# A fused attention and gated-MLP block on one core: first loads in another order, six split projections, and a new instruction order

## The chip, the cores and the metric

The kernel runs on one NeuronCore of a Trainium2 chip. The metric is device time in microseconds for one launch. Names of engines: PE is the matrix engine (PEld its weight loads), DVE the vector engine, ACT the scalar engine, POOL GpSimd, SP the engine that issues most transfers. ACT can issue transfers too.

## The reference

Sequence 2048, width 512, all in bf16. `layernorm` has no scale or shift.

```python
q, k, v = split(layernorm(x) @ wqkv)            # 32 heads of 16
# each position looks at 8 keys: itself and 2, 4, ..., 14 positions back
logits = einsum("bhsd,bhswd->bhsw", q, k_gathered) * 16 ** -0.5
attn = softmax(where(idx >= 0, logits, -1e9))
h = x + einsum("bhsw,bhswd->bhsd", attn, v_gathered) @ wo
g = layernorm(h) @ W_gate                        # 512 -> 1376
return h + (relu(g) * (layernorm(h) @ W_up)) @ W_down
```

## The kernel before, in words

The sequence is cut into four chunks (tk = 0 to 3) of 512 rows, each of four blocks of 128 rows. All weights and x stay in on-chip memory once loaded (`x_sm`, `wqk_sb`, `wv_sb`, `wo_sb`, `wgu_sb`, `wd_sb`). A chunk passes these steps; the letters are the keys of the steps in the code, with a chunk's number behind a dot in the text.

- Layer norm of x: `xst` and `xag` (statistics and aggregate on DVE, L454 and L457), `xrl` and `xre` (two small steps on ACT, L467 and L471), `xn` (normalised rows, DVE, L489), `xtp` (four 128-column transposes per block on PE, L518), `xte` or `xtv` (copy out of the accumulator bank, on ACT L534 or DVE L532). In chunk 0 each block goes through this by itself; blocks 0 and 2 are copied by ACT, 1 and 3 by DVE.
- Projections: twelve outputs of 128 x 512 (four each of q, k, v), each of four matmuls over the depth of 512 (`dt` = 0 to 3, L559), and a copy by ACT (`qe`, L567).
- Scores: DVE multiplies q with shifted k (`pr`, L608, in halves in chunk 0, L623), PE sums within heads (`sc`, L614), ACT takes the exponential, PE sums the denominators (`den`). The weights are spread over the head's rows by transfers on SP (`bd`, L732; on PE, `bc`, L743, in chunk 0).
- Values: DVE multiplies with shifted v (`mu`, L764, L779), an accumulating transfer issued by POOL adds the upper to the lower half (`ta`, L807; in chunk 3 DVE does this), DVE adds the rest (`tree`, L767, L801; `om`, L771, in chunk 0). The result is OT; PE multiplies with wo (`wo`, L833), the sum with x goes back into `x_sm` (`rs`).
- Second layer norm (`hnm`, `hsq`, `hrl`, `hre`, `hxn`) with transposes on PE (`htp`) or by transfers on SP (`htd`, L507).
- MLP: up and gate matmuls (`mm`, L906), copies on ACT (`ue` L910, `ge` L913), a product on DVE (`gu`, L934), the down projection (`dn`, L952), a last sum with x (`o`, L963) and the store (`os`).

All these steps are recorded first (`plan.add`) with their engine, what they depend on and the buffers that they take. `Plan.order` then lists them engine by engine: `RANK` gives each of the 737 steps its place, and a planner, with a duration for each step and a landing time for each load (`xload`, `wload`), decides what is written next; two pairs in `GUIDE` add dependences between first-chunk statistics. The engines run their lists in order, and every wait is by semaphore. The planner's numbers decide only the order.

The first loads are issued by hand in `setup`. x of chunk 0 goes in four pieces of 128 KB, the q, k weights in four pieces of 256 KB (one for each `dt`), half of each on SP and half on ACT. POOL holds back a later load by writing one element into its destination, in an instruction that reads an earlier load: `wv_sb` waits in that way for the first x (L326), chunk 2 for chunk 1 (L328).

Before the first transposes PE runs `NWARM` matmuls on a zero tile (L408), and after those of blocks of the first half `NFILL` more (L416). The first four projections of chunk 0 are cut in three pieces each: columns 0 to 255 over the first half of the depth (`qka`), columns 256 to 511 over the first half (`qkc`), all columns over the second half (`qkd`).

```python
f_mm(lo, hi, 0, 2)      # qka and qkc: two matmuls of 256 columns
f_mm(0, CS, 2, NT)      # qkd: two matmuls of 512 columns
```

Of the kernel before, what the change touches and what calls it, by code (L numbers as in the profile page):

```python
# [16 lines left out]

RANK = [
    0, 1, 2, 3, 4, 5, 6, 7, 8, 9, 10, 11, 12, 13, 14, 15, 16, 17, 19, 20,
    25, 27, 32, 39, 18, 21, 23, 24, 26, 30, 40, 42, 29, 34, 36, 37, 41, 43, 46, 22,  # L20
    28, 31, 33, 35, 38, 44, 49, 53, 56, 66, 47, 60, 71, 85, 48, 54, 58, 62, 45, 50,
    51, 55, 77, 82, 72, 78, 81, 101, 68, 89, 100, 110, 61, 69, 96, 102, 94, 114, 107, 70,
    116, 111, 126, 135, 145, 99, 74, 95, 105, 112, 117, 120, 169, 183, 196, 149, 164, 156, 153, 159,
    123, 133, 138, 130, 128, 207, 199, 213, 234, 237, 241, 185, 162, 191, 223, 233, 240, 189, 194, 200,
    230, 235, 238, 170, 147, 176, 203, 211, 220, 250, 258, 256, 261, 246, 252, 243, 248, 266, 276, 264,
    273, 267, 271, 263, 269, 279, 282, 286, 290, 289, 292, 296, 293, 297, 291, 294, 300, 330, 335, 319,
    321, 308, 312, 316, 323, 338, 353, 357, 340, 355, 334, 342, 343, 360, 364, 304, 309, 325, 328, 314,
    333, 310, 336, 348, 356, 365, 337, 347, 349, 362, 327, 345, 367, 346, 384, 359, 371, 368, 377, 363,
    369, 388, 376, 382, 392, 373, 386, 390, 402, 381, 431, 450, 465, 415, 445, 475, 489, 403, 429, 459,
    466, 411, 424, 448, 485, 67, 73, 59, 65, 52, 64, 57, 63, 75, 76, 83, 88, 79, 86, 93,  # L30
    80, 91, 84, 90, 97, 174, 198, 157, 168, 142, 195, 172, 206, 151, 179, 106, 109, 115, 122, 132,
    221, 136, 143, 108, 118, 103, 113, 119, 125, 215, 225, 232, 254, 242, 249, 260, 265, 274, 278, 281,
    284, 295, 288, 302, 322, 332, 358, 370, 331, 339, 372, 383, 341, 350, 380, 385, 317, 324, 361, 378,
    397, 406, 393, 396, 395, 400, 389, 394, 408, 410, 399, 405, 404, 407, 398, 401, 412, 413, 418, 421,
    414, 417, 419, 423, 416, 422, 425, 436, 439, 438, 444, 457, 481, 447, 472, 488, 451, 462, 432, 442,
    443, 460, 453, 458, 464, 461, 469, 476, 487, 474, 478, 468, 483, 490, 486, 493, 482, 491, 463, 495,
    514, 519, 523, 522, 527, 524, 535, 508, 533, 504, 536, 539, 513, 532, 544, 517, 530, 547, 549, 541,
    582, 647, 681, 543, 607, 616, 678, 531, 614, 624, 649, 537, 634, 638, 724, 87, 104, 124, 144, 129,
    139, 131, 137, 152, 163, 177, 182, 175, 180, 186, 181, 187, 178, 188, 192, 201, 210, 227, 229, 253,
    259, 226, 247, 222, 231, 208, 245, 239, 244, 205, 214, 228, 251, 277, 311, 270, 374, 285, 344, 298,  # L40
    275, 315, 318, 268, 257, 280, 326, 352, 354, 366, 375, 387, 379, 391, 440, 449, 480, 484, 427, 434,
    456, 479, 420, 428, 454, 467, 433, 441, 471, 477, 499, 507, 492, 496, 497, 502, 494, 498, 510, 512,
    500, 503, 505, 509, 501, 506, 515, 516, 525, 538, 528, 534, 518, 521, 520, 526, 566, 570, 557, 571,
    569, 581, 604, 608, 613, 563, 567, 575, 580, 561, 564, 573, 583, 585, 546, 551, 556, 558, 550, 555,
    553, 560, 565, 628, 630, 601, 611, 621, 626, 618, 622, 633, 625, 639, 597, 632, 578, 588, 610, 637,
    644, 631, 635, 643, 629, 640, 641, 645, 667, 670, 673, 676, 658, 688, 716, 721, 636, 669, 671, 674,
    684, 685, 694, 723, 134, 140, 121, 127, 92, 98, 141, 146, 148, 150, 160, 166, 155, 165, 173, 154,
    161, 158, 167, 171, 262, 283, 184, 209, 236, 303, 190, 204, 272, 287, 217, 219, 218, 255, 197, 202,
    212, 224, 301, 305, 299, 307, 193, 216, 313, 306, 320, 329, 409, 351, 426, 430, 435, 437, 446, 452,
    470, 455, 473, 529, 540, 545, 552, 554, 568, 572, 579, 511, 562, 574, 577, 542, 548, 559, 576, 584,  # L50
    587, 586, 591, 589, 595, 593, 599, 590, 592, 594, 596, 598, 600, 602, 603, 605, 606, 620, 623, 609,
    612, 615, 617, 619, 627, 642, 656, 680, 683, 675, 691, 648, 661, 692, 682, 700, 687, 689, 696, 702,
    690, 697, 706, 654, 679, 664, 666, 665, 668, 672, 677, 686, 652, 660, 657, 659, 646, 650, 653, 655,
    662, 699, 710, 707, 709, 704, 713, 693, 711, 714, 651, 698, 701, 663, 695, 703, 705, 715, 717, 719,
    720, 708, 722, 726, 730, 718, 725, 728, 732, 729, 733, 735, 736, 712, 727, 731, 734,
]


# [33 lines left out]
class Plan:  # L92
# [18 lines left out]
        return op  # L111


    GUIDE = (("xag0", 0, "xst1", 0), ("xxn1", 0, "xst2", 0))

    def order(self):
        for kx, cx, ky, cy in self.GUIDE:
            xs = [o for o in self.ops if o.key and o.key[0].startswith(kx) and o.key[1] == cx]
            for o in self.ops:
                if o.key and o.key[0].startswith(ky) and o.key[1] == cy:  # L120
                    o.deps = o.deps + xs
        waiting = list(self.ops)
        free = {}
        queues = None
# [84 lines left out]
def kernel(  # L209
# [11 lines left out]
    nc = tc.nc  # L221
# [83 lines left out]
    def setup():  # L305

        w3_r = A_wqkv.rearrange("(dt p) f -> p dt f", p=P)
        for j in range(BPC):
            (nc.scalar if j % 2 else nc.sync).dma_start(x_sm[:, j:j + 1, :], x_rows[:, j:j + 1, :])
        for dt in range(NT):  # L310
            (nc.scalar if dt % 2 else nc.sync).dma_start(wqk_sb[:, dt:dt + 1, :], w3_r[:, dt:dt + 1, 0:2 * D])
        nc.sync.dma_start(x_sm[:, BPC:2 * BPC, :], x_rows[:, BPC:2 * BPC, :])
        nc.scalar.preload_act_table_set("natural_log_exp_and_others")
        V.memset(warm[:], 0.0)
        make_identity(nc, identity[:])
# [7 lines left out]
        nc.gpsimd.memset(vT[:, :, 0:PADL], 0.0)  # L323


        nc.gpsimd.tensor_copy(out=wv_sb[0:1, 0, 0:1], in_=x_sm[0:1, 0, 0:1])  # L326
        nc.sync.dma_start(wv_sb[:], w3_r[:, :, 2 * D:3 * D])
        nc.gpsimd.tensor_copy(out=x_sm[0:1, 2 * BPC, 0:1], in_=x_sm[0:1, BPC, 0:1])  # L328
        for tk in range(2, NCK):
# [33 lines left out]
    DAC2 = ()  # L363
    PRS, MUH = (0,), (0,)
    TDD, TDL = 1.25, 1.5
    NWARM, NFILL = 44, 8
    DMAT = (('h',2,0),('h',2,2),('h',3,0),('h',3,2),('h',1,0))

    EARLY = (1, 2, 3)
# [27 lines left out]
    def load(t):  # L397
        return add(None, "LD", 0.0, None, lat=t)

    xload = [[load(t) for t in (3.5, 3.7, 4.1, 4.35)]] + [[load(t)] * BPC for t in (10.8, 14.4, 17.8)]  # L400
    wload = {n: load(t) for n, t in
             (("q", 9.55), ("k", 9.55), ("ab", 8.1), ("v", 12.1), ("o", 19.2), ("u", 22.6), ("g", 26.1), ("d", 30.1))}

    wb = Buf(bank_s)

# [1 line left out]
        for _ in range(NWARM):  # L407
            nc.tensor.matmul(wb.t[:, 0:P], lhsT=warm[:], rhs=warm[:], start=True, stop=True)  # L408

    fills = [add(("warm", 0), "PE", 5.7, f_warm, [], -500, take=[wb])]  # L410

    def fill(d):

# [128 lines left out]
    for tk in range(NCK):  # L542
# [10 lines left out]
        for n, (c, t) in enumerate(seq):  # L553
            mm = Buf(mm_s)
            pr = base + 10 + 0.1 * n

            def f_mm(lo=0, hi=CS, d0=0, d1=NT, c=c, t=t, mm=mm, xnT=xnT):
                for dt in range(d0, d1):
                    nc.tensor.matmul(mm.t[:, lo:hi], lhsT=wv_sb[:, dt, t:D:NT] if c == 2 else wqk_sb[:, dt, c * D + t:(c + 1) * D:NT],  # L559
                                     rhs=xnT.t[:, dt, lo:hi], start=(dt == 0 and lo == 0), stop=(dt == NT - 1))  # L560

            def f_ev(c=c, t=t, mm=mm, qT=qT, s0=s0):
                if c == 0:
                    o = qT.t[:, t, :]
                else:
                    o = (kT if c == 1 else vT)[:, t, PADL + s0: PADL + s0 + CS]
                nc.scalar.copy(out=o, in_=mm.t[:])  # L567

            wl = wload["qkv"[c]]
            if tk == 0 and n < 4:  # L570

                ab, done = [wload["ab"]], []
                for i, (lo, hi, evs) in enumerate(((0, 2 * P, xev[0:2]), (2 * P, CS, xev[2:]))):
                    done.append(add(("qk%s%d" % ("ac"[i], n), tk), "PE", 2 * MM * (hi - lo) / CS + 0.005,
                                    lambda f=f_mm, lo=lo, hi=hi: f(lo, hi, 0, 2), evs + ab + done + [fills[-1]], pr - 5,
                                    take=[mm], use=[xnT]))
                a = add(("qkd%d" % n, tk), "PE", 2 * MM, lambda f=f_mm: f(0, CS, 2, NT), done + [wl], pr - 4.9, take=[mm],
                        use=[xnT], lat=PEL)
            else:
                a = add(("qkv%d" % n, tk), "PE", 4 * MM, f_mm, xev + [wl], pr, take=[mm], use=[xnT], lat=PEL)  # L580
            b = add(("qe%d" % n, tk), "ACT", A5, f_ev, [a], pr, take=[qT] if c == 0 else [], use=[mm], lat=AL)
            if c == 0:
                qd[t] = b
            elif c == 1:
                kdone[tk, t] = b
            else:
                vd[t] = b
# [434 lines left out]
```

## Time and profile before

| what | value |
|---|---|
| timed runs, median of 3 (lowest to highest) | 198.19 us (198.18 to 198.19) |
| span of the profiled execution, first to last instruction | 196.6 us |
| busy time of PE in the span | 190.5 us, 97% |
| busy time of DVE | 154.0 us, 78% |
| busy time of ACT | 111.7 us, 57% |
| granted clock of PE, mean | 1.000 |
| moved by transfers | 21.99 MB, mean 112 GB/s |
| start of the first projection matmul | 8.76 us |

The profile is of one execution; the timed runs are others of the same program, so the two are compared by differences. A busy PE counts matmuls that overlap, with modelled ends, so the pace of matmuls is taken from many of a kind in a row. In lines of the timeline the first two numbers are start and length in us, "x8" counts instructions, and the bracket tells how long the engine was idle ahead and what ended that.

### The profile page before, as it was taken

To read this page: it belongs to the slowest core of one execution; us is meant where nothing else is said; L and a number is where in the kernel's file an instruction comes from. 1 tells how busy PE (TensorE), PEld (TensorE's weight loads), DVE (VectorE), ACT (ScalarE), POOL (GpSimd) and SP (SyncE) were. 2 spreads that over 40 slices of the span, in tenths; PEclk is the share of its full clock that TensorE was granted. 3 is DMA by queue.
4 is the path that set the end of the run, shared out by engine and by line. 5 is a ranking of instruction groups with operands and counts; after the bars stand their busy time and mean duration, and the time that the engine had idled before them with its cause. 6 is when DMAs were issued, how large, how long until landed. Compare 5 with 4: busy or idle time off the path is not lost.

```text
span 196.6 us, 3034 instructions
## 1 busy us (share of the span) xinstructions
PE 190.5 (97%) x1111; PEld 97.1 (49%) x1131; DVE 154.0 (78%) x251; ACT 111.7 (57%) x234; POOL 12.7 (6%) x28
## 2 busy tenths in 40 slices
PE   7899999999999999999999999999999999999994
PEld 7756445654445434464444435444444655444542
DVE  6779999999999999999999779999686331223233
ACT  3548699984598947694334658505674615235400
POOL 4000000330000013100033000000000000000000
PEclk9999999999999999999999999999999999999999
DMA  6969980695000809947369971411002220030114
GB/s 154 310 202 389 405 262 2 122 198 108 3 0 6 196 15 173 188 89 169 81 130 198 181 204 64 82 29 24 3 0 53 53 57 0 0 107 0 27 57 133
DMA packets 21134, 21.99 MB, mean 112 GB/s; under 512 B 8736, under 2 KB 17920, under 8 KB 21120
## 3 DMA queue, kind: packets, MB, share of 16 engines
q1 hardware_dynamic: 18672, 14.65, 25.9%
q0 software_dynamic: 1728, 6.29, 17.2%
q10 hardware_dynamic: 720, 0.85, 1.4%
q8 instruction: 9, 0.15, 0.3%
q14 instruction: 5, 0.04, 0.1%
HBM read 8.42 MB, written 2.10 MB: 53 GB/s over the span
## 4 chain that ended last, share of the span: by engine, by line
PE 66%; DMA 14%; issue 13%; DVE 4%; POOL 1%; SPq 1%; POOLq 0%; DVEq 0%
PE bank L906 20%; PE bank L559 19%; PE bank L952 14%; DMA big<-big 7%; PE bank L833 5%; DMA wv_sb<-in_A_wqkv_dram 4%; PE bank L614 2%; DVE big L764 2%; PE bank L873 2%; PE bank L518 2%; DMA x_sm<-in_A_x_dram 1%; POOL big L807 1%; DMA big<-ex 1%; DVE big L608 1%; PE bank L836 1%
## 5 line engine op out<-in xcount | busy, mean ns | idle before, releaser
L906 PE MATMUL bank<-quad,wgu_sb 128*128 128x512 bf16 x313 | 72.0, 379 | 0.4
L906 PEld LDWEIGHTS <-wgu_sb 128*128 128x128 bf16 x320 | 31.0, 98 | 37.3 <-issue 0.8
L952 PE MATMUL bank<-wd_sb,gT 128*128 128x512 bf16 (+2 forms) x182 | 40.1, 366 | 0.3
L913 ACT ACTIVATE gr<-bank 128x512 bf16<-128x512 f32 x40 | 23.2, 603 | 26.0 <-PE bank L906 24.5
L910 ACT CAST up_sb<-bank 128x512 bf16<-128x512 f32 x40 | 23.2, 594 | 16.5 <-PE bank L906 14.0
L934 DVE TENSOR_TENSOR gT<-gr,up_sb 128x1024 bf16<-128x1024 bf16 x20 | 13.7, 689 | 22.7 <-ACT up_sb L910 16.8
L559 PE MATMUL bank<-quad,wqk_sb 128*128 128x512 bf16 (+1 forms) x132 | 30.2, 367 | 0.2
L952 PEld LDWEIGHTS <-gT 128*128 128x128 bf16 (+1 forms) x187 | 18.1, 98 | 19.5 <-issue 0.4
L764 DVE TENSOR_TENSOR big<-big,vT 128x4096 bf16<-128x4096 bf16 x12 | 27.0, 2283 | 0.1
L608 DVE TENSOR_TENSOR big<-quad,kT 128x4096 bf16<-128x4096 bf16 x12 | 27.0, 2284 | 0.0
L559 PEld LDWEIGHTS <-wqk_sb 128*128 128x128 bf16 x136 | 14.7, 114 | 13.0 <-issue 2.1
L963 DVE TENSOR_TENSOR row<-x_sm,bank 128x512 bf16<-128x512 bf16 (+1 forms) x17 | 10.8, 651 | 9.2 <-PE bank L952 9.2
L767 DVE TENSOR_TENSOR big<-big 128x1024 bf16<-128x1024 bf16 (+2 forms) x24 | 16.8, 729 | 1.2 <-DMA big<-big 1.2
L559 PE MATMUL bank<-quad,wv_sb 128*128 128x512 bf16 x62 | 15.7, 380 | 0.4 <-DMA wv_sb<-in_A_wqkv_dram 0.3
L807 POOL DMA_DIRECT2D big<-big x12 | 10.5, 874 | 85.0 <-DVE big L764 55.0
L833 PE MATMUL bank<-wo_sb,quad 128*128 128x512 bf16 x62 | 14.7, 379 | 0.4 <-DVE quad L801 0.3
L489 DVE TENSOR_SCALAR row<-x_sm,mv,rs 128x512 bf16<-128x512 bf16 x32 | 11.4, 407 | 1.8 <-ACT rs L471 1.8
L534 ACT COPY quad<-bank 128x1024 bf16<-128x1024 bf16 (+1 forms) x11 | 10.0, 944 | 4.5 <-PE bank L518 4.4
L567 ACT CAST kT<-bank 128x512 bf16<-128x512 f32 x16 | 8.9, 598 | 5.7 <-PE bank L559 5.5
L454 DVE BATCH_NORM_STATS2 st<-x_sm 128x6 f32<-128x512 bf16 x16 | 10.3, 675 | 2.1 <-DMA x_sm<-in_A_x_dram 2.1
L567 ACT CAST quad<-bank 128x512 bf16<-128x512 f32 x16 | 9.5, 607 | 3.6 <-PE bank L559 3.6
L443 ACT ACTIVATE row<-x_sm,mv 128x512 bf16<-128x512 bf16 x12 | 8.6, 714 | 4.2 <-DVE mv L435 4.0
(72 smaller groups left out, 157.5 us busy)
## 6 DMA issues: line engine op xcount, KB each, us to landing
big<-big POOLq DMA_DIRECT2D x12, 512.0 KB, 5.4
big<-ex SPq DMA_DIRECT2D x24, 128.0 KB, 2.7
out_dram<-row SPq DMA_DIRECT2D x15, 128.0 KB, 1.8
x_sm<-in_A_x_dram SPq DMA_DIRECT2D x3, 512.0 KB, 4.9
wgu_sb<-in_B_W_up_dram SPq DMA_DIRECT2D x1, 1376.0 KB, 8.8
wgu_sb<-in_B_W_gate_dram SPq DMA_DIRECT2D x1, 1376.0 KB, 11.8
wd_sb<-in_B_W_down_dram SPq DMA_DIRECT2D x1, 1280.0 KB, 15.2
wqk_sb<-in_A_wqkv_dram SPq DMA_DIRECT2D x2, 256.0 KB, 6.9
```

What stands on the lines that cost most here:

```text
L559: nc.tensor.matmul(mm.t[:, lo:hi], lhsT=wv_sb[:, dt, t:D:NT] if c == 2 else wqk_sb[:, dt, c * D + t:(c + 1) * D:NT], rhs=xnT.t[:, dt, lo:h ...
L567: nc.scalar.copy(out=o, in_=mm.t[:])
L608: V.tensor_tensor(out=pb.t[:].rearrange("p (t w) s -> p t w s", t=2), in0=q4, in1=k4, op=ALU.mult)
L764: V.tensor_tensor(out=mt.t[:], in0=ab.t[:], in1=v8, op=ALU.mult)
L767: V.tensor_tensor(out=mt.t[:, 0:n, :], in0=mt.t[:, 0:n, :], in1=mt.t[:, n:2 * n, :], op=ALU.add)
L807: nc.gpsimd.dma_start(mt.t[:, 0:4, :], mt.t[:, 4:8, :], accum_op=ALU.add)
L833: nc.tensor.matmul(od.t[:], lhsT=OT.t[:, t, j * P:(j + 1) * P], rhs=wo_sb[:, t, :], start=(t == 0), stop=(t == NT - 1 and tk not in RPE))
L906: nc.tensor.matmul(mm.t[:fs, lo:hi], lhsT=wgu_sb[:, dt, g, ft * P: ft * P + fs], rhs=hnT.t[:, dt, lo:hi], start=(dt == 0), stop=(dt == NT ...
L910: nc.scalar.copy(out=ub.t[:fs, i, :], in_=um.t[:fs, :])
L913: nc.scalar.activation(out=gr.t[:fs, i, :], in_=gm.t[:fs, :], func=ACT.Relu)
L934: V.tensor_tensor(out=gt.t[:fs, 0:n, :], in0=gr.t[:fs, 0:n, :], in1=ub.t[:fs, 0:n, :], op=ALU.mult)
L952: nc.tensor.matmul(od.t[:, c0:c1], lhsT=gts[ft].t[:fs, ft % 2, j * P:(j + 1) * P], rhs=wd_sb[:fs, ft, c0:c1], start=(ft == 0), stop=(ft == ...
```

## The change

- **First loads.** On both queues a piece of x is followed by a weight piece: SP has x0, w0, x2, w2, ACT has x1, w1, x3, w3 (before: x0, x2, w0, w2 and x1, x3, w1, w3). The x of chunk 1, issued before right behind these, is now held by POOL until x3 has landed; `wv_sb` is held until w3 has landed (before: x0).
- **Projections.** Six of chunk 0 instead of four are split, each in two: columns 0 to 255 over the full depth (`qka`, four matmuls of 256 columns) and columns 256 to 511 over the full depth (`qkc`). Both need all four weight pieces.
- **Warming.** 38 matmuls instead of 44.
- **Order.** `GUIDE` is gone, the planner's landing times and one duration are others, and `RANK` is a new list.

On PE this makes 10 pairs of weight load and matmul more (16 more for the projections, 6 fewer for warming). In DVE's list for chunk 0 `xn` of block 0 now stands ahead of the statistics of block 3, and `xn` of block 1 behind them. The first entries of the two lists (chunk 0), before and after:

```
DVE before: xst0 xag0 xst1 xag1 xst3 xn0 xn1 xag3 xst2 xag2 xn3 xn2 xtv1 xtv3
DVE after:  xst0 xag0 xst1 xag1 xn0 xst3 xn1 xag3 xst2 xtv1 xag2 xn3 xn2 xtv3
PE before:  warm xtp0 xtp1 fill xtp3 fill xtp2 qka3 qka1 qka2 qka0 qkc3 qkd3 qkc0 qkc2 qkd0 qkd2 qkc1 qkv9
PE after:   warm xtp0 fill xtp1 fill qka4 qka2 xtp3 qka1 xtp2 qka0 qka3 qkc3 qkc2 qka5 qkc1 qkc5 qkc4 qkv7 qkv6
```

```diff
 RANK = [
     0, 1, 2, 3, 4, 5, 6, 7, 8, 9, 10, 11, 12, 13, 14, 15, 16, 17, 19, 20,
-    25, 27, 32, 39, 18, 21, 23, 24, 26, 30, 40, 42, 29, 34, 36, 37, 41, 43, 46, 22,
+    22, 25, 27, 28, 18, 21, 23, 24, 29, 32, 35, 36, 31, 37, 40, 41, 43, 47, 50, 26,
...
-    GUIDE = (("xag0", 0, "xst1", 0), ("xxn1", 0, "xst2", 0))
-
...
-        for kx, cx, ky, cy in self.GUIDE:
-            xs = [o for o in self.ops if o.key and o.key[0].startswith(kx) and o.key[1] == cx]
-            for o in self.ops:
-                if o.key and o.key[0].startswith(ky) and o.key[1] == cy:
-                    o.deps = o.deps + xs
...
-        for j in range(BPC):
-            (nc.scalar if j % 2 else nc.sync).dma_start(x_sm[:, j:j + 1, :], x_rows[:, j:j + 1, :])
-        for dt in range(NT):
-            (nc.scalar if dt % 2 else nc.sync).dma_start(wqk_sb[:, dt:dt + 1, :], w3_r[:, dt:dt + 1, 0:2 * D])
-        nc.sync.dma_start(x_sm[:, BPC:2 * BPC, :], x_rows[:, BPC:2 * BPC, :])
+        for i in range(2):
+            for n, q in enumerate((nc.sync, nc.scalar)):
+                j = 2 * i + n
+                q.dma_start(x_sm[:, j:j + 1, :], x_rows[:, j:j + 1, :])
+                q.dma_start(wqk_sb[:, j:j + 1, :], w3_r[:, j:j + 1, 0:2 * D])
...
-        nc.gpsimd.tensor_copy(out=wv_sb[0:1, 0, 0:1], in_=x_sm[0:1, 0, 0:1])
+        nc.gpsimd.tensor_copy(out=x_sm[0:1, BPC, 0:1], in_=x_sm[0:1, 3, 0:1])
+        nc.sync.dma_start(x_sm[:, BPC:2 * BPC, :], x_rows[:, BPC:2 * BPC, :])
+        nc.gpsimd.tensor_copy(out=wv_sb[0:1, 0, 0:1], in_=wqk_sb[0:1, 3, 0:1])
         nc.sync.dma_start(wv_sb[:], w3_r[:, :, 2 * D:3 * D])
...
-    NWARM, NFILL = 44, 8
+    NWARM, NFILL = 38, 8
+    NHALF = 6
+    XT = (3.35, 3.55, 5.3, 5.6, 9.3, 14.4, 17.8)
+    WT = (7.4, 7.4, 5.8, 11.8, 19.2, 22.6, 26.1, 30.1)
...
-                                     rhs=xnT.t[:, dt, lo:hi], start=(dt == 0 and lo == 0), stop=(dt == NT - 1))
+                                     rhs=xnT.t[:, dt, lo:hi], start=(dt == 0 and lo == 0), stop=(dt == NT - 1 and hi == CS))
...
-            if tk == 0 and n < 4:
-
-                ab, done = [wload["ab"]], []
+            if tk == 0 and n < NHALF:
+
+                a = None
                 for i, (lo, hi, evs) in enumerate(((0, 2 * P, xev[0:2]), (2 * P, CS, xev[2:]))):
-                    done.append(add(("qk%s%d" % ("ac"[i], n), tk), "PE", 2 * MM * (hi - lo) / CS + 0.005,
-                                    lambda f=f_mm, lo=lo, hi=hi: f(lo, hi, 0, 2), evs + ab + done + [fills[-1]], pr - 5,
-                                    take=[mm], use=[xnT]))
-                a = add(("qkd%d" % n, tk), "PE", 2 * MM, lambda f=f_mm: f(0, CS, 2, NT), done + [wl], pr - 4.9, take=[mm],
-                        use=[xnT], lat=PEL)
+                    a = add(("qk%s%d" % ("ac"[i], n), tk), "PE", 4 * MM * (hi - lo) / CS + 0.005,
+                            lambda f=f_mm, lo=lo, hi=hi: f(lo, hi), evs + [wl, a, fills[-1]], pr - 5,
+                            take=[mm], use=[xnT], lat=PEL if i else 0.0)
```

## The prediction

> **What bounds the kernel now.** I read the page first, then the stages, then the start and the one late wait in the timeline. All times are those of the one profiled execution: its span is 196.6 us, the timed runs have a median of 198.19, so 1.6 us lie around the span; I take that as unchanged and forecast by differences. About 0.2% (0.4 us) is what a measurement of this kernel can tell from no change.
>
> ```profile
> span 196.6 us, 3034 instructions
> ...
> PE 190.5 (97%) x1111; PEld 97.1 (49%) x1131; DVE 154.0 (78%) x251; ACT 111.7 (57%) x234; POOL 12.7 (6%) x28
> ```
>
> PE is busy 97% of the span. The table by stages says where the rest is (columns: length, busy time of PE, PEld, DVE, ACT, POOL, granted clock, DMA share, GB/s):
>
> ```profile
> 0.00:10.00 10.00, 8.39 (x86) 7.65 (x88) 6.90 (x26) 4.33 (x11) 2.02 (x15) 1.00 0.78 233
> ...
> 20.00:40.00 20.00, 19.89 (x142) 10.37 (x143) 20.00 (x36) 17.71 (x35) 2.52 (x3) 1.00 0.63 195
> ...
> 100.00:120.00 20.00, 19.57 (x90) 8.72 (x90) 17.57 (x33) 11.18 (x23) 2.58 (x3) 1.00 0.89 185
> ...
> 140.00:160.00 20.00, 19.89 (x102) 9.72 (x102) 11.38 (x29) 11.20 (x25) 0.00 (x0) 1.00 0.16 33
> ```
>
> From 20 us on PE idles 0.1 to 0.2 us in 20, except in 100 to 120, where it idles 0.43. So time can come only from the start and from that one wait, and DVE, fully busy from 13 us to about 103, must come forward with PE or PE waits for it. The start, by the timeline (start, length, engine, line, idle before):
>
> ```profile
> 0.99 4.61 PEld L408 LDWEIGHTS <-warm 128*128 128x128 bf16 x44 [0.99 <-DVE warm L314]
> ...
> 5.05 0.69 DVE L454 BATCH_NORM_STATS2 st<-x_sm 128x6 f32<-128x512 bf16 x1
> ...
> 5.67 0.72 DVE L489 TENSOR_SCALAR row<-x_sm,mv,rs 128x512 bf16<-128x512 bf16 x2
> ...
> 6.11 0.55 PEld L518 LDWEIGHTS <-row 128*128 128x128 bf16 x8 [0.51 <-DVE row L489]
> ...
> 6.62 0.49 PEld L416 LDWEIGHTS <-warm 128*128 128x128 bf16 x8
> ...
> 8.20 0.75 DVE L532 COPY quad<-bank 128x512 bf16<-128x512 bf16 x2
> ...
> 8.76 3.21 PE L559 MATMUL bank<-quad,wqk_sb 128*128 128x256 bf16 x21
> ...
> 10.87 1.88 DVE L454 BATCH_NORM_STATS2 st<-x_sm 128x6 f32<-128x512 bf16 x3 [1.92 <-DMA x_sm<-in_A_x_dram]
> ...
> 12.22 1.05 PE L559 MATMUL bank<-quad,wv_sb 128*128 128x512 bf16 x4 [0.26 <-DMA wv_sb<-in_A_wqkv_dram]
> ```
>
> PE has no real work until 6.11, the first projection starts at 8.76, and at 12.22 PE has just waited for wv_sb. DVE stands idle 1.92 us until the x of chunk 1 lands. The late wait:
>
> ```profile
> 114.04 0.69 DVE L767 TENSOR_TENSOR big<-big 128x1024 bf16<-128x1024 bf16 x1 [1.16 <-DMA big<-big]
> ...
> 115.25 3.14 PEld L833 LDWEIGHTS <-quad 128*128 128x128 bf16 x16 [0.82 <-DVE quad L801]
> ```
>
> **The start, step by step.** x0 and x1 stay first on their queues, so they land as now, 3.34 and 3.53 (issue 0.74 and 0.73, landing 2.6 and 2.8 later). DVE now goes from the second statistics straight to xn of block 0, so that begins at 5.05, where the third statistics begin today; transposes follow 0.44 later (5.67 to 6.11 today), at 5.49. The 38 warming matmuls, at 4.61/44 = 0.105 each, end at 5.0 and hide under that.
>
> Behind xn of block 0 stands the statistics of x3, and xn of block 1 waits behind it. x3 lands today at 1.17 + 3.9 = 5.07 and x2 at 3.97. In the changed kernel 2 x 256 KB of q, k weights lie ahead of the two. At the 363 GB/s of 3.0 to 3.5 us that is 1.4 us on x2's 3.97, about 5.4. At the rate of the dip it would be 3.4 us, so up to 8.4:
>
> ```profile
> 3.00:3.50 0.50, 0.50 (x7) 0.50 (x6) 0.33 (x3) 0.50 (x1) 0.10 (x1) 1.00 1.04 363
> ...
> 4.50:5.00 0.50, 0.50 (x7) 0.50 (x6) 0.47 (x2) 0.38 (x2) 0.00 (x0) 1.00 1.18 166
> 5.00:5.50 0.50, 0.50 (x8) 0.50 (x6) 0.50 (x2) 0.36 (x2) 0.00 (x0) 1.00 0.75 139
> ...
> 7.00:7.50 0.50, 0.28 (x6) 0.11 (x2) 0.47 (x3) 0.24 (x2) 0.00 (x0) 1.00 1.10 367
> ```
>
> The engines are as busy in the dip, but move half as much. It follows SP's issues of chunk 1 (3.54) and wv_sb (4.05), and the change moves both behind the first wave. So I take 5.5 for x3, near the fast end, and keep 5.1 to 8.4 as bounds.
>
> From there: statistics 0.65, xn 0.33, aggregate 0.1, statistics of x2 0.62, then the copy of block 1 (0.38; its transposes are done by then), 0.1 to PE: the projections start 2.2 us after x3 lands, at 7.7 to 7.8. All four weight pieces must be in, since the first matmuls now go over the full depth. They land at 8.16, 8.26, 9.5 and 9.65 today (issue 1.66 to 2.15, landing 6.5 to 7.5 later). The first wave is 1.57 MB; the mean rate up to 8 us (204 GB/s) carries it by 7.9 even with the dip, and at 363 from 2 us on by 6.3. With 0.4 for completion: 6.7 to 8.3; I take 7.3, hidden behind 7.8.
>
> PE's first projection moves from 8.73 to 7.8, but two of the four transposes (0.45 us: 8 x 0.057) are still ahead of PE then, so 0.48 is gained. The second gain is the wait for wv_sb: 16 matmuls of 256 columns at 0.109 and 6 of 512 at 0.216 fill 8.76 to 11.80, PE goes on at 12.22, so 0.42. In the new order wv_sb is first used after 6 + 5 halves (4.8), two whole projections (1.7), and six sets of four transposes, at 15.7; issued at 7.6, it would have 8 us where the later 512 KB loads take 3.5 to 4.9. Behind wv_sb on SP queue only chunks 2, 3 and the later weights, none needed before 20 us. The 16 extra pairs of load and matmul cost nothing as long as 256 columns keep their 0.109. PE gains 0.90.
>
> DVE's side: after the last copy (9.5) come chunk 1's statistics, if that x is in. It is issued after x3 (about 5.9); the later chunk loads took 3.5 and 4.9, so 9.4 to 10.8, today 10.84. I take 9.5: DVE gains 1.37 and is no brake. The first tight place is sc1 of chunk 0: PE's work ahead of it shrinks from 14.8 to 12.2 us, so PE comes at 19.6; DVE's last pr step ahead of it is done at 19.3: four statistics (0.62), four aggregates (0.09), four xn (0.33) and five half products (1.13) are 9.8, from 9.5.
>
> **The late wait.** L833 of chunk 2 stands after 107.27 us of PE's own work in the new order, 105.72 today (counted down its queue: 0.216 per 512 columns, as 39 matmuls take 8.42 in the chain; 0.109, 0.057, 0.98 per sc step). PE would come unstalled at 114.76 today, so at 114.76 + 1.55 - 0.90 = 115.4. DVE's first product for chunk 2 stands 0.66 us earlier in its order and the ex copies for chunk 3 1.6 us later, so the four accumulating transfers, which with those copies hold the DMA share at 0.89 in 100 to 120, start earlier and share less; DVE's last OT step comes near 113.6. The wait of 114.76 to 115.25 goes: 0.49. Next late is DVE's hn chain of chunk 2: its last xn now stands behind a 2.2 us product, the four DMA transposes end about 13.9 after L833 begins, PE needs them 14.5 after.
>
> The rest of the new order moves work between places that have slack today; PE's total is the same to 0.02 us. For ties (wo of chunk 0, the four transposes after it, wo of chunk 1, each under 0.3 us of slack) I charge 0.15, bounds 0 and 1.2. Sum: -0.48 - 0.42 - 0.49 + 0.15 = -1.24, so 196.95, say 197.0.
>
> **The rivals.**
> - Slower, x behind weights. If the dip belongs to the weights and not to SP's issues, x3 lands late, and DVE's in-order queue holds xn of block 1 behind it. Each us costs PE a us: the sum is zero at x3 = 6.8. At 7.4 it is +0.6: 198.8. For: the dip (172, 166, 139 GB/s from 4.0 to 5.5) comes when the x is nearly through and the weights are what moves. Against: from 3.5 to 4.0, with weights moving already, it was still 248.
> - Chunk 1's x no earlier than today. DVE gains nothing, PE waits at sc1, and about 0.15 + 0.49 - 0.15 is left: 197.7. For: it is still behind all of the first wave on SP. Against: wv_sb no longer follows at its heels.
> - New waits in the new order, the hn transposes of chunk 2 above all: 0.6 to 1.2 lost, 197.6 to 198.2.
> - PE slow at the start. The warm loads run at 0.105 each (44 in 4.61), the fills after 6.6 at 0.06 (8 in 0.49): PE doubles its pace between. Six fewer warming matmuls and a gap of 0.45 before the first transposes could put that off. If 1.4 us of projections ran at the old pace, 0.7 is lost: 197.65. [...]
>
> **How the numbers follow.** Forecast as worked out 0.50; x behind weights 0.17; late chunk 1 0.15; new waits 0.12; slow PE 0.06. Faster by over 0.2% (below 197.79): nearly all of the first, two thirds of the third, half of the fourth and fifth: 0.68. Within 0.2%: 0.16. Slower: most of the second: 0.16. Low end: x3 at 5.1, no new waits, 196.5. High end: the slower rival at 198.8.
>
> **What would show it.** Right: first L559-type matmul at 7.7 to 7.9, no idle at the first wv_sb matmul, chunk 1's statistics at 9.5, no PE idle at wo of chunk 2, a span near 195.4. Wrong: DVE idle before the third statistics past 6.8; PE idle at sc1 of chunk 0; PE idle before the first L906-type matmuls of chunk 2; projections 0.216 apart at 256 columns.

## The result, and the profile after

The changed kernel took 199.85 us in the median of 16 executions (198.18 to 201.94), the kernel before 198.17 of 16 (197.83 to 199.49). The ratio is 1.0053 [1.0027, 1.0079]: slower, where 197.0 was forecast. Medians here are over all executions; the ratios leave out the longest of those with a lower clock.

The 16 fall in two groups. Nine had a mean granted clock of 0.998 to 1.000 and took 198.2 to 200.1; seven had 0.991 and took 200.3 to 201.9. The unchanged kernel was run twice more (e4, e13), 40 executions in all:

| kernel | executions | mean clock under 0.995 | median of the others | their median span |
|---|---|---|---|---|
| before (five later occasions) | 113 | none | 198.17 us | 196.4 us |
| changed (199.85, 198.24, 199.10) | 40 | 13, median 200.76 us | 198.62 us | 196.6 us |

The mean clock leaves out the time before the full clock is first granted: one execution of a later kernel (e3) has a mean of 1.000, though its full clock came only at 10.44 us. So an execution with a late grant is not among the 13.

So two things are to be explained: at the full clock the forecast gain of 1.24 us is missing and 0.45 lost, and every third execution loses some 2 us more.

The profile of the changed kernel is of an execution of 198.52 us at a clock of 0.999, so one that kept its clock. The head of its page:

```profile
span 196.5 us, 3056 instructions
...
PE 190.0 (97%) x1122; PEld 98.3 (50%) x1141; DVE 153.8 (78%) x251; ACT 112.1 (57%) x234; POOL 12.8 (7%) x29
```

The span is 0.1 us shorter, PE has its extra pairs. The table by stages (length, busy time of PE, PEld, DVE, ACT, POOL, clock, DMA share, GB/s):

```profile
0.00:10.00 10.00, 7.85 (x85) 7.34 (x86) 7.22 (x27) 3.95 (x11) 2.36 (x17) 1.00 0.70 221
...
20.00:40.00 20.00, 19.84 (x141) 10.48 (x137) 20.00 (x39) 17.21 (x36) 2.73 (x3) 1.00 0.74 204
40.00:60.00 20.00, 19.73 (x113) 9.40 (x114) 19.00 (x22) 14.73 (x35) 0.86 (x1) 1.00 0.21 40
60.00:80.00 20.00, 19.68 (x139) 9.08 (x140) 19.38 (x15) 13.42 (x28) 2.58 (x3) 1.00 0.49 103
...
100.00:120.00 20.00, 19.89 (x104) 9.62 (x103) 17.14 (x28) 11.57 (x21) 2.58 (x3) 1.00 0.85 179
```

The kernel before between 40 and 80:

```profile
40.00:60.00 20.00, 19.89 (x114) 9.49 (x115) 20.00 (x24) 14.40 (x35) 1.08 (x2) 1.00 0.36 69
60.00:80.00 20.00, 19.84 (x136) 9.05 (x138) 20.00 (x16) 14.62 (x29) 2.59 (x3) 1.00 0.52 107
```

PE's idle time between 100 and 120 is gone, as forecast. It is back between 40 and 80 (0.59 us for 0.27), and DVE, which was busy for 20.00 of 20.00 us in both of those stages, now idles 1.6 us there. The start, by the timeline:

```profile
5.12 0.38 DVE L486 TENSOR_SCALAR row<-x_sm,mv,rs 128x512 bf16<-128x512 bf16 x1
...
5.81 0.69 DVE L451 BATCH_NORM_STATS2 st<-x_sm 128x6 f32<-128x512 bf16 x1 [0.31 <-DMA x_sm<-in_A_x_dram]
...
7.40 0.41 DVE L529 COPY quad<-bank 128x512 bf16<-128x512 bf16 x1
...
7.95 1.04 PE L556 MATMUL bank<-quad,wqk_sb 128*128 128x256 bf16 x8 [0.24 <-DVE mv L454]
...
9.59 2.47 DVE L451 BATCH_NORM_STATS2 st<-x_sm 128x6 f32<-128x512 bf16 x4
...
15.77 0.17 PEld L556 LDWEIGHTS <-wv_sb 128*128 128x128 bf16 x2
```

In this execution the start runs nearly as the forecast had it: xn of block 0 at 5.12 (5.05), the third statistics at 5.81, the first projection 2.14 later (2.2), chunk 1's statistics at 9.59 (9.5), no wait for wv_sb. Then come the new waits (PE, PE, ACT, PE):

```profile
48.55 1.05 PE L609 MATMUL bank<-big,sel 128*32 128x512 bf16 x16 [0.17 <-ACT kT L564]
...
62.54 1.38 PE L515 MATMUL bank<-identity,row 128*128 128x128 bf16 x16
...
78.41 1.07 ACT L905 CAST up_sb<-bank 128x512 bf16<-128x512 f32 x2 [3.07 <-DVE gT L929]
...
79.04 0.59 PE L687 MATMUL bank<-ex,same 128*128 128x512 bf16 x2 [0.21 <-ACT up_sb L905]
```

The 16 transposes at 62.54 take 1.21 us to the next matmul where 16 x 0.057 is 0.91. And the idle stretches of DVE (with the ACT steps ahead of two of them and behind one), its last OT step of chunk 2 (L796) and PE's weight loads for wo behind it:

```profile
42.38 2.05 ACT L564 CAST kT<-bank 128x512 bf16<-128x512 f32 x4 [0.83 <-PE bank L556]
...
42.99 2.29 DVE L603 TENSOR_TENSOR big<-quad,kT 128x4096 bf16<-128x4096 bf16 x1 [0.88 <-ACT kT L564]
...
47.91 0.58 ACT L564 CAST kT<-bank 128x512 bf16<-128x512 f32 x1 [2.36 <-DVE big L603]
...
71.02 6.70 DVE L759 TENSOR_TENSOR big<-big,vT 128x4096 bf16<-128x4096 bf16 x3 [0.62 <-DMA big<-ex]
...
107.40 0.58 ACT L905 CAST up_sb<-bank 128x512 bf16<-128x512 f32 x1 [1.13 <-PE bank L901]
...
109.04 0.43 DVE L711 TENSOR_TENSOR ex<-ex,rec 128x512 bf16<-128x512 bf16 x1 [1.34 <-ACT rec L693]
...
115.05 0.42 DVE L796 TENSOR_TENSOR quad<-big 128x512 bf16<-128x512 bf16 x1
...
116.28 2.69 PEld L828 LDWEIGHTS <-quad 128*128 128x128 bf16 x13
```

In the kernel before that OT step was at 114.77:

```profile
114.77 0.42 DVE L801 TENSOR_TENSOR quad<-big 128x512 bf16<-128x512 bf16 x1
```

DVE's lead of 1.28 us at chunk 1's statistics has gone into 0.88 + 0.62 of waiting, for a kT copy for which ACT itself waits on a matmul of PE, and for the ex transfers. Summed from matmul to matmul, less the gaps that both kernels have, PE's new waits are 0.24 (sc of chunk 1), 0.28 (the transposes), 0.43 (den of chunk 2 and the step behind it) and 0.10 (131 us): 1.05. In e4, a second profile of the same kernel, they are 0.86, with no wait at den.

### The profile page after: what moved, and what is told of

It is laid out like the page before. It is cut to its first block, busy times and chain, and to the rows that moved or that the text cites. A ratio compares the mean times of both kernels' runs of the same rounds, so it can differ in the third digit from the quotient of the medians.

```text
span 196.5 us, 3056 instructions
## 1 busy us (share of the span) xinstructions
PE 190.0 (97%) x1122; PEld 98.3 (50%) x1141; DVE 153.8 (78%) x251; ACT 112.1 (57%) x234; POOL 12.8 (7%) x29
## 4 chain that ended last, share of the span: by engine, by line
PE 82%; DVE 5%; DMA 4%; ACT 3%; issue 3%; ACTq 0%; DVEq 0%
PE bank L901 30%; PE bank L947 19%; PE bank L556 17%; PE bank L828 7%; PE bank L609 3%; PE bank L515 2%; PE bank L868 2%; DVE big L603 2%; DMA x_sm<-in_A_x_dram 2%; DMA big<-ex 2%; ACT big L744 2%; DVE big L759 2%; PE bank L687 1%; ACT kT L564 1%; PE bank L831 0%
## 5 line engine op out<-in xcount | busy, mean ns | idle before, releaser
L947 PE MATMUL bank<-wd_sb,gT 128*128 128x512 bf16 (+2 forms) x185 | 40.6, 366 | 0.2
L556 PE MATMUL bank<-quad,wqk_sb 128*128 128x512 bf16 (+1 forms) x148 | 29.7, 345 | 0.5 <-DVE mv L454 0.2
L556 PEld LDWEIGHTS <-wqk_sb 128*128 128x128 bf16 x152 | 16.3, 114 | 10.9 <-issue 1.9
L556 PE MATMUL bank<-quad,wv_sb 128*128 128x512 bf16 x62 | 14.9, 379 | 0.1
L556 PEld LDWEIGHTS <-wv_sb 128*128 128x128 bf16 x64 | 7.1, 114 | 6.2 <-issue 0.4
```

The source lines that it names most:

```text
L947: nc.tensor.matmul(od.t[:, c0:c1], lhsT=gts[ft].t[:fs, ft % 2, j * P:(j + 1) * P], rhs=wd_sb[:fs, ft, c0:c1], start=(ft == 0), stop=(ft == ...
```

## The experiments

Theories: **O**, the new order's waits use up what the start gains; **C**, the clock comes late or is lost when PE idles in the first 10 us; **X**, what makes it idle is x block 3, landing late behind weight pieces; **D**, DVE sets the time of chunk 2's output projections, so an earlier PE only waits there; **S**, the new kernel takes longer outside its span.

### Warming, loads, and the same kernel again

```diff
 # e1: f_warm of the changed kernel     # e2: f_warm of the kernel before
-        for _ in range(NWARM):          -        for _ in range(NWARM):
+        for _ in range(44):             +        for _ in range(38):
 # e3: the kernel before with the changed kernel's loads in setup; e4: the changed kernel
```

> The changed kernel with 44 warming matmuls issued instead of 38, order untouched. Of 16 executions of the changed kernel 7 had a mean granted clock of 0.991 and took 200.3 to 201.9 us, 9 had 0.998 to 1.000 and took 198.2 to 200.1. Theory C (PE's clock is released later when the warming stops early): the executions at 0.991 become rare, at most 2 in 10, and the median falls from 199.9 to 198.5 to 199.0. Theory O (the new order waits, the clock has nothing to do with the warming): still 4 in 10 at 0.991, median 199.5 or more.

> The kernel before with 38 warming matmuls issued instead of 44, all else as it was. Theory C: some 4 in 10 executions at 0.991, each about 1.7 us longer, so the median or the mean rises by 0.7 to 1.7 us. Theory O: no difference from before, within 0.2 us.

> The kernel before with the changed kernel's first loads alone (order, projections and 44 warming matmuls as before). The statistics of block 3 stand ahead of both xn in this order and x3 lands at 5.7 instead of 5.05, so the projections start near 9.1 instead of 8.76; wv_sb no longer makes PE wait at 12.2, and DVE starts chunk 1 about 1 us earlier. Theory O: the loads by themselves do no harm, 197.4 to 198.2, and no wider spread than before. If the loads are what spreads the times: over 198.6, with a spread of 2 us or more.

> The changed kernel once more, beside the others on the same chip. Both theories: a median of 199 to 200.5. Theory C: executions at 0.991 are 1.5 us or more above those at 0.998 to 1.000, and where the profiled execution is one of them, PE's matmuls keep the pace of 0.107 us for 128 columns about 3.4 us longer than in the first profile, into the projections.

Measured, beside 198.13 for the kernel before: e1 198.29 (197.83 to 199.25), ratio 1.0009 [0.9991, 1.0027]; e2 198.29, 1.0006 [0.9987, 1.0025]; e3 199.73, 1.0078 [1.005, 1.0107]; e4 198.24, 1.0011 [0.9991, 1.0031]. At 0.991 or less: 0 of 12, 1 of 12, 4 of 10 and 1 of 12.

The same kernel is at 198.24 here and was at 199.85; the executions at the low clock are 1 of 12 here and were 7 of 16. C's numbers hold in e1 but not in e2: in the old kernel 38 warming matmuls cost one low execution of 12 and 0.16 us in the median, not 4 in 10 and 0.7. O's number fails in e3: the new loads by themselves, under the old order, are slow. In e3's trace x3 lands at 6.3, PE idles 1.79 us from 5.61, and the full clock comes only at 10.44 (5.75 in the kernel before). e2 shows something else: its PE has no wait for wv_sb, but waits 0.71 at chunk 2's wo in place of 0.49. In the old order the 0.42 at wv_sb was not all to be had; a PE that is earlier is stopped at that wo.

Each set also gives the time outside the span, which I had taken as unchanged: 1.79 for the kernel before and 1.77 for e2, 2.05 and 2.06 for e1 and e4, 2.18 for e3.

### Old order behind the new start; less and more warming; alternating loads alone

```diff
 # e5: RANK up to the second score sum of chunk 0 as changed, then the old lists; 44 warming
 # e6: range(30) in f_warm    # e7: range(44) in f_warm, and
-            for _ in range(NFILL):
+            for _ in range(14):
 # e8: the kernel before, first eight loads alternating, nothing else
```

> The changed kernel's loads, half-width projections and order up to the second score sum of chunk 0 (bc0.0 on PE, mu3c.0 on DVE, the last be0.0 on ACT), then the per-engine order of the kernel before; 44 warming matmuls. Theory O (the new order's own waits, about 0.9 us of PE between 48 and 131 us, use up what the start gains): without that order the waits at 48.0, 62.5 to 63.8, 78.5 and 130.8 us are gone, the last matmul starts 0.5 to 0.9 us earlier than in the kernel before (193.4), span 195.4 to 195.9, time 197.4 to 198.0. Rival D (the gain of the start cannot be used, because DVE is the bound from 20 to 115 us): the wait at the output projections of chunk 2 grows from 0.49 to about 1 us, span 196.1 to 196.5, time 198.1 to 198.6.

> The changed kernel with 30 warming matmuls in place of 38; nothing else. They end near 4.1 us and the first transposes come at 5.55 us, so that TensorE is idle for 1.4 us in place of 0.6. [...] Rival N (the clock does not hang on the warming): like the changed kernel of the last set, median 198.1 to 198.4 with at most 2 of 12 above 199.

> The changed kernel with 44 warming matmuls in place of 38 and 14 in place of 8 in each of the two groups of fill matmuls behind the first two pairs of transposes; nothing else. TensorE is then busy from 1.0 us to the first projection but for about 0.3 us. Theory C: no execution at a mean clock of 0.991, all but one or two within 0.5 us of the lowest, median 198.0 to 198.3. Rival N: the share of long executions is that of the changed kernel.

> The kernel before with its first eight loads alternating between x blocks and weight pieces; the second chunk's x and the v weights are issued as before, with no copy ahead of x. The executions of the changed kernel so far are 2.0 to 2.1 us longer than their span, those of the kernel before 1.7 to 1.9 us. Theory S1 (the order of the first loads makes that difference): 2.0 to 2.2 us here. Theory S2 (the two chained copies on POOL ahead of the second chunk's x and of the v weights make it): 1.7 to 1.9 us. For the span: the weights land earlier than with the copies' loads in place before, x of chunk 0 later; 196.5 to 198.5.

Beside 198.26: e5 198.45, 1.002 [0.9997, 1.0043]; e6 200.95 of 6, 1.0148 [1.0119, 1.0177]; e7 199.26, 1.003 [1.001, 1.0049]; e8 201.31 of 3, 1.0145 [1.0112, 1.0178]. Low clock: 1 of 12, 3 of 6, 0 of 12, 3 of 3.

O fails its number: with the old order e5 is no faster than e4 (lowest span 196.0 and, on another chip, 195.9). Its time is in D's range, but the wait at chunk 2's wo is 0.44 in its trace, not D's 1 us. C holds for 30 warming matmuls (3 of 6 at the low clock and a median of 200.95, where rival N had 198.1 to 198.4); two more executions of e6 took 200.99 and 201.30 at a clock of 1.000, and no trace tells why. e7 lost no clock, but 7 of its 12 took over 199.2; its trace (x3 at 6.44, projections at 8.59) shows a late start instead, in an execution of 198.81. e8 is the plainest case of X: x3 at 7.48, PE idle for 2.93 us, clock lost, 1.81 outside the span. S1 (the load order makes the time outside) falls with that.

### x first again

```diff
-        for i in range(2):
-            for n, q in enumerate((nc.sync, nc.scalar)):
...
+        for j in range(BPC):
+            (nc.scalar if j % 2 else nc.sync).dma_start(x_sm[:, j:j + 1, :], x_rows[:, j:j + 1, :])
+        for dt in range(NT):
+            (nc.scalar if dt % 2 else nc.sync).dma_start(wqk_sb[:, dt:dt + 1, :], w3_r[:, dt:dt + 1, 0:2 * D])
...
-        nc.gpsimd.tensor_copy(out=x_sm[0:1, BPC, 0:1], in_=x_sm[0:1, 3, 0:1])
+        nc.gpsimd.tensor_copy(out=x_sm[0:1, BPC, 0:1], in_=wqk_sb[0:1, 1, 0:1])
 # e9: in the changed kernel with 44 warming; e10: in e5; e11, e12: these two without
 # the copy that holds wv_sb
```

> The changed kernel with 44 warming matmuls, its first eight loads in the old order (the four x blocks of chunk 0 first, then the four weight pieces, in turn on SP and ACT), and the second chunk's x held behind weight piece 1 in place of x block 3. Theory X (with alternating loads, x blocks 2 and 3 land behind weight pieces at a time that differs by over 1 us between executions: statistics of x block 3 began at 5.8, 5.7, 7.0, 6.4 and 7.5 us in the traces so far; TensorE idles meanwhile and then loses its clock for 3.4 us): x block 3 is there by 4.7 us as in the kernel before, the projections begin at 7.6 to 8.1 us when the weights land, no execution has a mean clock of 0.991, all but two lie within 0.6 us of the lowest; median 197.6 to 198.2. Rival W (the weights land later behind x, as in the kernel before, where the projections began at 8.76): projections at 8.7 or later, median 198.6 to 199.2.

> The loads of e9 with the order of e5 (the changed kernel's order to the end of the second score sum of chunk 0, then that of the kernel before). Theory O (the new order's waits of about 0.9 us use up the start's gain): 0.4 to 0.9 us less than e9, span 195.2 to 195.7, no wait of TensorE above 0.3 us. Rival D (DVE is the bound until its last work on chunk 2, so that an earlier start of TensorE is given back at that chunk's output projections): a wait of 0.9 us or more there, span as in e9 within 0.3 us.

> e9 without the copy on POOL that holds the v weights' load behind weight piece 3; the v weights follow the second chunk's x on SP. POOL has then as many copies as in the kernel before. Theory S2 (the time outside the span, 1.75 to 1.8 us in the kernel before and 2.0 to 2.2 with one more chained copy, hangs on the number of these copies): 1.75 to 1.9 us outside the span, and 0.2 to 0.4 us less than e9. Rival S3 (it hangs on a load held behind a weight piece at all): 2.0 us or more outside. The weights of chunk 0 or the second chunk's x could land later by up to 0.5 us.

> e10 with the single copy of e11. By theories O and S2 together the fastest of these, 197.0 to 197.6; by D and S3 as e9.

Beside 198.16, six executions each: e9 199.50, 1.0073 [1.005, 1.0096]; e10 199.59, 1.0067 [1.0047, 1.0087]; e11 200.10, 1.0091 [1.0062, 1.0121]; e12 199.92, 1.0084 [1.0065, 1.0103].

None of the 24 had a low clock, which is X's part. The times are above the ranges of X and of rival W. The projections begin at 7.5 to 7.9, as X had it, but the last weight piece's packets end at 7.7 to 8.4 (7.2 in the first profile and e4): inside the first projections PE waits 0.28 us in e9, 0.33 in e11 and 0.97 in e10 and e12. Chunk 1's x, held behind a weight piece, lands only at 10.6 to 11.6, and PE waits 0.26 to 0.66 us more before chunk 1's transposes.

On O against D, e9 and e10 are alike but for the order: 199.50 and 199.59, with intervals of some 0.4 us on each side. That is D's equal time and not O's 0.4 to 0.9 us (single traces do not decide it: e10's lost 0.69 us more than e9's at the weights). What the traces show is an exchange. The gap of 0.33 us before sc of chunk 1 and the three gaps of 0.1 us within the transposes behind it stand in all twelve traces of the new order, however its start went, and in none of the eight whose order is the old one at that place. The old order has this one instead:

```profile
116.23 1.04 PE L827 MATMUL bank<-wo_sb,quad 128*128 128x512 bf16 x4 [0.49 <-DVE quad L795]
```

From matmul to matmul it is 0.65 in e10 and 0.50 in e12 (D had 0.9 or more). S2 (the number of copies on POOL makes the time outside) fails: with one copy less, e11 still has 2.19 us outside.

### One step of DVE; holding chunk 1's x; the new order without the new loads

```diff
 # e13: the changed kernel.  e14: RANK values 26 and 29 exchanged: xn of block 1
 # goes ahead of the statistics of block 3
-    22, 25, 27, 28, 18, 21, 23, 24, 29, 32, 35, 36, 31, 37, 40, 41, 43, 47, 50, 26,
+    22, 25, 27, 28, 18, 21, 23, 24, 26, 32, 35, 36, 31, 37, 40, 41, 43, 47, 50, 29,
 # e15: changed kernel, chunk 1's x issued behind the first eight loads, not held
-        nc.gpsimd.tensor_copy(out=x_sm[0:1, BPC, 0:1], in_=x_sm[0:1, 3, 0:1])
 # e16: kernel before with that copy and chunk 1's load behind it
 # e17: changed kernel with the old loads.  e18: e14 with 44 warming
```

> The changed kernel, unchanged, as the base for e14 and e15 on the same chip. From its 28 executions so far: 1 to 6 of 12 at a mean clock of 0.991, the lowest at 198.0 to 198.3, 2.0 to 2.1 us outside the span, median 198.2 to 199.9.

> The changed kernel with one step moved on DVE: the normalisation of x block 1 goes ahead of the statistics of x block 3. Theory X (a late x block 3 holds DVE's in-order queue, so the second transposes come late, TensorE idles and loses its clock for 3.4 us): the second transposes come near 6.2 us wherever x block 3 lands, at most 1 of 12 executions at 0.991, median 198.0 to 198.4, at least 0.1 us lower than e13 if e13 has 2 or more such executions. Rival Z (the clock is lost for the shorter warming or for late weights, not for x block 3): the same share at 0.991 as e13, median within 0.1 us of it or above, since x block 3's statistics begin 0.3 to 0.5 us later where it lands early.

> The changed kernel without the copy that holds the second chunk's x behind x block 3: that load is issued on SP right behind the first eight. Theory S4 (that copy makes the 0.3 us outside the span): 1.7 to 1.9 us outside. Rival S5 (something else in the changed kernel makes them): 2.0 to 2.2. For the span: the second chunk's x then shares the transfers with x block 3 and the weights, which land up to 1.2 us later (as they did in e8: block 3 at 7.5, weights at 8.3), so 196.5 to 199.5 with more executions at 0.991 than e13.

> The kernel before with one thing changed: the second chunk's x is held behind x block 3 by a copy on POOL. S4: 2.0 to 2.2 us outside the span; S5: 1.7 to 1.9. For the span: the weights land up to 1 us earlier than 9.05, so that the projections begin near 8.0 to 8.8; what is gained there goes into the wait at the output projections of chunk 2 if DVE is the bound (rival D of e5): span 196.0 to 196.6.

> The changed kernel with the loads of the kernel before (x blocks first, the second chunk's x right behind them, nothing held but the v weights behind x block 0); half-width projections, 38 warming matmuls and the new order stay. Theory X and S (the lost clock and the 0.3 us outside the span both come with the loads): no execution at 0.991, 1.75 to 1.85 us outside the span; the weights land near 9.0, the projections begin at 8.7 to 9.1, so that the span is 196.6 to 197.3 by the new order's waits of 0.7 to 1.0 us, time 198.4 to 199.1. Rival P (the new order or the shorter warming loses the clock): 2 or more of 12 at 0.991.

> e14 with 44 warming matmuls in place of 38. Theory X: as e14 (198.60 there) or up to 0.3 us lower, as the clock is granted more surely; 198.2 to 198.6, not below the kernel before, since the 0.3 us outside the span stay.

Beside 198.18 (e13 to e16) and 198.15:

| run | median | ratio | low clock | outside the span |
|---|---|---|---|---|
| e13 changed | 199.10 | 1.0057 [1.0034, 1.008] | 5 of 12 | 2.04 |
| e14 xn of block 1 first | 198.60 | 1.0021 [1.0011, 1.0031] | 0 of 12 | 2.08 |
| e15 chunk 1's x not held | 201.05 | 1.0119 [1.0083, 1.0154] | 5 of 6 | 2.05 |
| e16 before, x held | 198.47 | 1.0009 [0.9995, 1.0023] | 0 of 11 | 2.16 |
| e17 changed, old loads | 199.29 | 1.006 [1.004, 1.0081] | 0 of 6 | 2.02 |
| e18 e14 with 44 warming | 198.77 | 1.0029 [1.001, 1.0048] | 0 of 12 | 2.05 |

e13's profile caught an execution of 202.1 us. Its timeline:

```profile
5.84 0.61 PE L413 MATMUL bank<-warm 128*128 128x128 bf16 x8
...
7.40 0.69 DVE L451 BATCH_NORM_STATS2 st<-x_sm 128x6 f32<-128x512 bf16 x1 [1.85 <-DMA x_sm<-in_A_x_dram]
...
8.46 0.61 PE L515 MATMUL bank<-identity,row 128*128 128x128 bf16 x4 [2.02 <-DVE row L486]
...
9.72 1.91 PE L556 MATMUL bank<-quad,wqk_sb 128*128 128x256 bf16 x8
```

DVE waits 1.85 us for x3 with xn of block 1 behind it in its list, PE idles 2.18 us after the fills, and eight 256-column matmuls take 1.91 us where the profile of the first set has 1.04. Two stretches of e13 by clock (the column after POOL's):

```profile
4.00:7.25 3.25, 1.49 (x24) 1.14 (x21) 1.48 (x5) 1.58 (x5) 0.00 (x0) 1.00 0.80 277
7.30:14.10 6.80, 5.64 (x37) 4.66 (x38) 4.91 (x12) 1.58 (x5) 0.58 (x3) 0.50 0.68 208
```

The clock is full from 3.88, half from 7.29 to 14.12, then full for the rest of the work. Its last matmul starts 3.62 us later than in the first profile (196.87 for 193.25). The late x3 is 1.59 of that (7.40 for 5.81), the step from there to the first projection 0.18 (2.32 for 2.14), and the 4.40 us of projections at half speed 2.2. Some 0.35 of these 3.97 comes back, most of it at den of chunk 2, where PE waits 0.11 in place of 0.38. So the late x3 by itself is 1.6 of the 3.6 us, and the clock most of the rest. e14:

```profile
6.18 0.40 PE L515 MATMUL bank<-identity,row 128*128 128x128 bf16 x4
...
6.62 0.70 DVE L451 BATCH_NORM_STATS2 st<-x_sm 128x6 f32<-128x512 bf16 x1 [0.49 <-DMA x_sm<-in_A_x_dram]
...
8.58 1.04 PE L556 MATMUL bank<-quad,wqk_sb 128*128 128x256 bf16 x8 [1.55 <-DVE mv L454]
```

x3 is late here too, but the second transposes come at 6.18, and the clock stays: PE idles 1.99 us in the first 3.41 us at the full clock, where e13, which kept it for just that long (3.88 to 7.29), has 2.12. On one chip 5 of 12 (e13) against 0 of 12 (e14) is X's result, not Z's; the median is 0.2 above X's range. The start is not mended: the copy of block 1 (L529) still stands behind the statistics of blocks 3 and 2, so the first projection waits 1.55. To move that copy as well was not tried. 44 warming matmuls on top (e18) gain nothing.

e17 has the new order with x on time (third statistics at 5.17) and no low clock, and still takes 199.29. That speaks against P (six executions only), and the new loads are not the whole loss: in its trace PE waits 1.09 us for weight pieces inside the first projections, and the gaps of the new order are all there.

e15 and e16 speak against each other on S: without the hold the changed kernel still has 2.05 outside, with it the old one has 2.16, and e17, with the old loads and holds, has 2.02. Only the old order without a held chunk 1 has 1.8 (the kernel before, e2, e8; e5, e10 and e12, old only from the second score sum on, have 2.14). No trace shows anything outside the span; what the 0.3 us are stays open. None of these kernels beats the kernel before.

## Why the prediction was wrong

Three steps of the sum failed: x3's landing stood in it as one number, the waits of the new order were charged at 0.15 us where 1.05 and 0.86 came, and the time outside the span, taken as unchanged, grew by 0.26.

**x3 was taken as one number.** "I take 5.5 for x3, near the fast end." The working from there held (first projection 2.2 us after x3: measured 2.14, 2.15, 2.15 in the first profile, e4 and e7), and so did the bounds 5.1 to 8.4 (the upper one is 3.4 on today's 5.07; on x2's 3.97, as the lower end was reckoned, it is 7.4). But x3 is no constant. In traces with the new loads its statistics begin at 5.7, 5.7, 5.7, 5.8, 6.3, 6.4, 7.0 and 7.4 (e4, e6, e1, the first profile, e3, e7, e5, e13), and in e14 and e18, where DVE waits for it behind xn of block 1, at 6.6 and 6.7 (with chunk 1's x not held 6.3 in e15 and 7.5 in e8). Its packets begin at 4.0 to 4.6 behind w1 on ACT's queue and take 0.7 to 2.4 us; with x ahead they were through by 4.65. So "x behind weights", given 0.17, is not another case beside the forecast but its spread; the sum took a value just ahead of its early end. What makes the transfer take so different a time was not found.

**The clock.** "If 1.4 us of projections ran at the old pace, 0.7 is lost", chance 0.06: such a loss was measured (eight 256-column matmuls take 1.91 us at the half clock in e13, 1.04 at the full one in the first profile), but it was taken as a rare case of late release. The clock is also lost again after it was granted: in e13 it is full from 3.88 to 7.29, for 3.41 us, and then half to 14.12, for 6.83. By that pace 3.41 us at half speed cost up to 1.7 us (my estimate; less where PE idles in them), and by the mean clock the loss happened in 13 of 40. Fewer warming matmuls have their share: with 44 and the new loads and DVE list it was 1 of 36 (e1, e5, e7), with 30 it was 3 of 6; only part of that is on one chip. In the one low execution of the changed kernel that was traced the two add up: a late x3 makes the second gap (1.00 us up to 7.29), the shorter warming the first (1.12 us from 4.48).

The first grant is no fixed time either: in the traces it comes anywhere from 3.67 to 6.75 us (3.88 in e13, 4.85 in the first profile, 5.75 in the kernel before), once at 10.44 (e3). In the first profile and in that of the kernel before, the full clock then holds for 191.15 us.

**DVE's chain.** "DVE's last OT step comes near 113.6": it came at 115.05, and 114.71 in e4. I carried the lead of the start through 100 us on the strength of "DVE gains 1.37 and is no brake" and did not walk the new list for what DVE waits for. It waits for PE, by way of ACT: 0.88 us at 42.99 for the kT copy, 1.34 us at 109.04 for `rec`, which stands in ACT's list behind copies of PE's outputs. From there to the OT step DVE is busy without a break. So in the new order that step follows PE: PE's weight loads for wo begin 1.24 us behind it in all twelve traces, in e13 too, where both are 3.6 us later. In the eight traces with the old order there PE waits for the step and begins 0.48 us behind it. The wait at chunk 2's wo did go (-0.49), but not because DVE was early: its step came 0.28 later than in the kernel before, and PE, at 116.28 for 115.25, later still. D is shown for the old order only.

**New waits.** Charged at 0.15 within bounds of 0 and 1.2; 1.05 and 0.86 measured, none at the three places named. The step that failed is "moves work between places that have slack today": the k projection whose copy DVE awaits at 42.99 comes too late for it. From there DVE's products run without a break to 47.82, ACT's next kT copy waits 2.36 us for the last of them, and PE's sc step of chunk 1, at 48.55, for that copy. This 0.33 us gap is in every trace of the order. By the traces, against the first profile of the kernel before: start -0.36 (7.95 for 8.76, less 0.45 of transposes), wv_sb -0.42, wo -0.49, new waits +1.05, in sum -0.22; the last matmul starts 0.19 earlier (193.25 for 193.44). e4: -0.48 - 0.42 - 0.49 + 0.86 = -0.53, measured -0.48 (192.96). Some 0.05 is not accounted for.

**Outside the span.** "1.6 us lie around the span; I take that as unchanged": 1.79 before, 2.05 after, +0.26 in the medians. It turns a profile 0.1 us shorter into a time that is longer.

Right were the start of an execution with an early x3, wv_sb, chunk 1's x, and that the wait at wo would go.

## What to carry to other kernels

A landing time read from one profile is a sample (x3's statistics began at 5.81 us in the first profile of this kernel, at 7.40 in e13): where an in-order engine waits for a transfer behind others, price the spread of that transfer, not its best value, and keep independent work ahead of it in the list. A gain at the start counts only if the engine that is busy without a break further on keeps its lead too: walk that engine's new list, and those that feed it, step by step, to the next place where the two meet (here waits of 0.88 and 0.62 us used up DVE's lead of 1.28). Compare several timed executions with their clocks before a profile is believed.

## What had not been expected of the hardware

- Six traces differ in the clock as in PE's idle time over the first 3.41 us after the grant, added up from matmul starts: with 1.99 (e14), 2.02 (e15) and 2.04 us (e6) the clock was kept, with 2.12 (e13), 2.14 (e5) and 2.49 (e8) it was lost. Ahead of a grant PE was busy for more of the time, but the share gives no clean border: it was 75% (e8) and 79% (e15) of the 3.41 us that a grant followed, while 3.41 us with 60% (e3) and 66% (e13) were followed by none, and neither were those of e3 with 77% (0.20 to 3.61, counted back from its grant).
- Where the clock was granted earlier, the warming ended sooner: 38 matmuls were through at 4.48 us in e13 (granted at 3.88), at 4.95 in the first profile (4.85). The gap behind them was 1.12 us in e13 and 0.60 in the first profile.
- The time outside the span is no constant of the chip: 1.8 or 2.0 to 2.2 us, by kernel, and within 0.13 us of the kernel's median in every execution.
